# Loading wk in a row on one queue, an earlier activation-table load, and one kv group masked alone, in a gated linear-attention and MLP kernel

## The chip, the cores and the metric

The kernel runs on one NeuronCore of a Trainium2 chip. The metric is the device time of one execution in microseconds (us). A core has five engines that run side by side and meet at semaphores: TensorE (PE, with its weight loads PEld), VectorE (DVE), ScalarE (ACT), GpSimd (POOL) and SyncE (SP). DMAs are issued here by SP and ACT, each in the order of its own instructions, and are carried by 16 DMA engines.

## What is computed

Two branches read the same x (2048 tokens of 640 values) and are mixed by a gate that is one number per token:

```python
g = sigmoid((x * gate_w).sum(-1, keepdims=True))
# A: linear attention, 32 heads of 20; phi(t) = where(t > 0, t + 1, exp(t)) + 1e-6
q, k, v = split(x @ wqkv)
kv = einsum("bhsd,bhse->bhde", phi(k), v);  z = phi(k).sum over tokens
a  = (phi(q) @ kv / (phi(q) . z + 1e-6)) @ wo
# B: LayerNorm, w1, gelu, shifts of channel groups by 1 or 2 tokens, w2, residual;
#    then LayerNorm, w3, gelu, w4, residual
out = g * a + (1 - g) * b
```

Inputs and output are bf16.

## The kernel before

The order of the work on each engine is the order in which the program is written (a manual schedule): nothing is moved by a planner. Semaphore waits follow from the data and from the buffers. TensorE runs through these stages: k projection, q projection, the g products (phi(k) transposed times x), the first part of the MLP with the kv products between, and then, tile by tile of 512 tokens, w2, w3, attention output and w4.

PSUM is handed out in four pairs of banks by `pair()` in turn, so the fifth pair that is asked for takes the place of the first and waits until that one has been read.

**The start.** wk (640 by 640) is loaded in five pieces of 128 rows, wk0 to wk4 (`load_wk`), x in chunks of 128 tokens. The projections need x transposed, `xT`. Chunks 2 to 15 get it from seven transposing DMAs on SP's queue (`load_xT`: chunk 2, chunk 3, then pairs, then the last four). Chunks 0 and 1 are loaded plainly and *turned* on TensorE: `turn(c, dcs, pt, copy)` multiplies pieces of the chunk by the identity into a PSUM pair, from where VectorE or ScalarE copies them into `xT`. VectorE copies pieces 0 and 1 by way of the pair `tp`, ScalarE pieces 2, 3 and 4 by way of the pair `warm`. SP issues x chunk 0, x chunk 1, wk1, wk3 and then the transposes and all later weights; ACT issues the gate weights `g5`, wk0, wk2, wk4, and then loads its activation table, which belongs to a one-element Exp (L208).

On TensorE: five filler matmuls of ones (`warmup`, L204), the gate weights turned (L210, whose result VectorE puts into a spare column of wk), a short filler, the turn of chunk 0 (L217), two more fillers of 512 and 256 columns, the turn of chunk 1, and then the k projection (`k_mm`, L191): for each piece dc of the contraction, two matmuls of 320 columns for chunk 0 and two for chunk 1, into `kps[0]` and `kps[1]`; from chunk 2 on chunk by chunk. `k_evac` takes each result out with ScalarE (L195, L183) and VectorE (L184, L185).

**The kv mask.** `kv_mm` (L428) computes the products for head groups 0 to 2 into one PSUM pair and for groups 3 to 5 into another. `kv_mask` (L436, and L441 for the last, narrower group) multiplies them by a block mask into `kvT` on VectorE, three groups at a time. Then `m_mm` (L450) multiplies groups 0, 1 and 2 of `kvT` by wo, each into a pair of its own, and the MLP's `w1_mm` (L395) follows.

Of the kernel before, what the change touches and what calls it, by code (L numbers as in the profile page):

```python
# [7 lines left out]
ACT = mybir.ActivationFunctionType  # L8
ALU = mybir.AluOpType
BF16 = mybir.dt.bfloat16  # L10
# [6 lines left out]
def kernel(  # L17
# [13 lines left out]
    nc = tc.nc  # L31
    P = 128
# [4 lines left out]
    TS = 512  # L37
    NT = S // TS
    CPT = TS // P
    DC = D // P  # L40
# [8 lines left out]
    GW = GH * Dh  # L49
    NG = 6  # L50
# [17 lines left out]
    def pair():  # L68
        return ps.tile([P, 2, 512], F32, name="pp")
# [28 lines left out]
    gate = const.tile([P, NCH], F32)  # L98
# [20 lines left out]
    sp, aq, gq = nc.sync, nc.scalar, nc.gpsimd  # L119

    def load_x(c0, c1, q=sp):
        q.dma_start(x_sb[:, c0:c1, 0:D], x2[c0 * P:c1 * P, :].rearrange("(c p) d -> p c d", p=P))
# [4 lines left out]
    def load_wk(q, dc):  # L127
        q.dma_start(wk_sb[:, dc, 0:D], A_wqkv[dc * P:(dc + 1) * P, D:2 * D])
# [1 line left out]
    load_x(0, 1)  # L130
    aq.dma_start(g5[:], gate_w.rearrange("(c p) -> c p", p=P))
    load_x(1, 2)
    load_wk(aq, 0)
    load_wk(sp, 1)
    load_wk(aq, 2)
    load_wk(sp, 3)
    load_wk(aq, 4)
    for c0, c1 in ((2, 3), (3, 4), (4, 6), (6, 8), (8, 10), (10, 12), (12, 16)):
        load_xT(c0, c1)
    sp.dma_start(wq_sb, wqkv_v[:, :, 0:D])  # L140
# [7 lines left out]
    for g in (0, 2):  # L148
# [8 lines left out]
                            base=0, pattern=[[-1, P]], channel_multiplier=1)  # L157
    for c in range(0, NCH, CPT):
# [3 lines left out]
                            base=0, pattern=[[-4, H]], channel_multiplier=1)  # L162
    nc.gpsimd.affine_select(out=hmask[:], in_=hmask[:], compare_op=ALU.is_ge, fill=0.0,
                            base=3, pattern=[[4, H]], channel_multiplier=-1)
# [3 lines left out]
                            base=0, pattern=[[-HP, 2], [-Dh, GH], [0, Dh]], channel_multiplier=1)  # L168
    nc.gpsimd.affine_select(out=bmask2[:], in_=bmask2[:], compare_op=ALU.is_ge, fill=0.0,
                            base=Dh - 1, pattern=[[HP, 2], [Dh, GH], [0, Dh]], channel_multiplier=-1)  # L170
# [16 lines left out]
    def k_mm(pt, c, dcs, first=0, last=DC - 1):  # L187
        for dc in dcs:
            for hf in range(2):
                n = HD + hf  # L190
                nc.tensor.matmul(pt[:, hf, 0:n], lhsT=xT[:, dc, c * P:(c + 1) * P],  # L191
                                 rhs=wk_sb[:, dc, hf * HD:hf * HD + n], start=(dc == first), stop=(dc == last))
# [4 lines left out]

    warm, tp = pair(), pair()
    kps = [pair(), pair()]
    one = nc.const_aps.tensor(1.0, (P, TS), BF16)  # L200

    def warmup(n, w=TS, pt=kps[1]):
        for i in range(n):
            nc.tensor.matmul(pt[:, 1, 0:w], lhsT=one[:, 0:P], rhs=one[:, 0:w], start=True, stop=True)  # L204

    nc.vector.memset(g5z[:], 0.0)
    nc.vector.tensor_copy(g5z[0:DC, :], g5[:])
    nc.scalar.activation(gate[:, 0:1], one[:, 0:1], ACT.Exp)  # L208
    warmup(5)
    nc.tensor.matmul(kps[0][:, 0, 0:DC], lhsT=g5z[:], rhs=ident[:, 0:DC], start=True, stop=True)  # L210
    warmup(1, P)
# [2 lines left out]
    def turn(c, dcs, pt, copy):  # L214
        a, n = min(dcs), len(dcs)
        for dc in dcs:
            nc.tensor.matmul(pt[:, 0, (dc - a) * P:(dc - a + 1) * P], lhsT=x_sb[:, c, dc * P:(dc + 1) * P],  # L217
                             rhs=ident[:], start=True, stop=True)
        copy(xT[:, a:a + n, c * P:(c + 1) * P], pt[:, 0, 0:n * P].rearrange("p (c s) -> p c s", c=n))  # L219

    turn(0, (1, 0), tp, nc.vector.tensor_copy)
    turn(0, (2, 3, 4), warm, nc.scalar.copy)
    warmup(1, TS)
    warmup(1, 2 * P)
    turn(1, (1, 0), tp, nc.vector.tensor_copy)
    turn(1, (2, 3, 4), warm, nc.scalar.copy)
    for dc in range(DC):
        for c in range(2):
            k_mm(kps[c], c, (dc,))
    for c in range(2):  # L230
        k_evac(kps[c], c)
    for c in range(2, NCH):
        pt = pair()
# [186 lines left out]
    def kv_mm(g0, g1):  # L420
        pt = pair()
        for g in range(g0, g1):
            for fc in range(DC):
                for v in range(2 if g < NG - 1 else 1):
                    q = 2 * g + v
                    h0, h1 = GH * q, min(GH * (q + 1), H)
                    c1, o = min(GW * q + HP, D), (g - g0) * GW
                    nc.tensor.matmul(pt[HP * v:HP * v + c1 - GW * q, 0, o:o + (h1 - h0) * Dh],  # L428
                                     lhsT=wv_sb[:, fc, GW * q:c1],
                                     rhs=gT[:, fc, 0:D].rearrange("p (j m) -> p j m", j=DC)[:, :, 4 * h0:4 * h1],  # L430
                                     start=(fc == 0), stop=(fc == DC - 1))
        return pt

    def kv_mask(g0, g1, pt):
        n, k = min(g1, NG - 1) - g0, 2 * Dh
        nc.vector.tensor_tensor(  # L436
            kvT[:, g0:g0 + n, 0:GW].rearrange("p g (r j) -> p g r j", j=DC),
            pt[:, 0, 0:n * GW].rearrange("p (g j r) -> p g r j", g=n, j=DC),
            bmask[:].rearrange("p (r j) -> p r j", j=DC).unsqueeze(1).broadcast_to([P, n, 4 * GH, DC]), op=ALU.mult)
        if g1 == NG:  # L440
            nc.vector.tensor_tensor(  # L441
                kvT[0:k, NG - 1, 0:k].rearrange("p (r j) -> p r j", j=DC),
                pt[0:k, 0, n * GW:n * GW + k].rearrange("p (j r) -> p r j", j=DC),
                bmask[0:k, 0:k].rearrange("p (r j) -> p r j", j=DC), op=ALU.mult)
# [24 lines left out]
    hx0 = w1_gelu(0, w1_split[2], w1_mm(0, w1_split[2]))  # L469
    den_hi(halves[1])  # L470
    kv_ps = [kv_mm(0, 3), kv_mm(3, NG)]
    for i in range(2):
        kv_mask(3 * i, 3 * i + 3, kv_ps[i])
    mps = [pair() for _ in range(3)]
    for g in range(3):
        m_mm(g, mps[g])
# [270 lines left out]
```

## Time and profile before

| | us |
|---|---|
| median of 3 runs | 260.62 (260.37 to 261.76) |
| the profiled execution | 261.01 |
| its span, first to last instruction | 259.3 |
| TensorE busy | 254.4 (98% of the span) |
| VectorE, ScalarE, GpSimd busy | 147.5, 108.0, 32.6 |
| first turn, second turn, first k matmul start at | 3.22, 4.37, 4.92 |
| first q matmul starts at | 27.3 |

The profile is of one execution. Times within it count from the start of its span; a line L191 is line 191 of the kernel before. The busy time of an engine counts its instructions, not its waits or its DMA issues. The chain of waits goes back from the last instruction to what released each step. A queue such as SPq shows the issuing of a DMA, not its transfer; the landing time counts from the start of the issue to the completion.

### The profile page before, as it was taken

The page shows a single profiled execution, that of the slowest core. Times are in us where ns is not written, and L with a number is a line of the kernel's source. Part 1 is how long each engine was busy: PE and PEld are TensorE (multiplying, and loading weights), DVE is VectorE, ACT ScalarE, POOL GpSimd, SP SyncE. Part 2 cuts the span into 40 slices and gives each one's busy share as a digit, 9 for nine tenths or more (in the row PEclk, how much of TensorE's full clock was granted, in tenths as well). Part 3 has the DMA queues.
Part 4 walks back from the last instruction along what each step waited for, and adds up shares of the span by engine and source line. Part 5 has one row for each costly group of instructions (what it writes and reads, how often), then busy time and mean ns, then how long its engine had stood idle before and what let it go on. Part 6 is the DMA issues. An engine that isn't in the chain of part 4 may idle for free.

```text
span 259.3 us, 4190 instructions
## 1 busy us (share of the span) xinstructions
PE 254.4 (98%) x1625; PEld 150.5 (58%) x1648; DVE 147.5 (57%) x273; ACT 108.0 (42%) x168; POOL 32.6 (13%) x86
## 2 busy tenths in 40 slices
PE   8999999999999999999999999999999999999995
PEld 4777555688854644565464566464565555465543
DVE  2588778799999987697300497600287610125132
ACT  3555444375797447431342323343321343342100
POOL 4000050023411230041000131000132000000000
PEclk9999999999999999999999999999999999999999
DMA  7999998025572787934011023212022401211011
GB/s 213 188 177 371 355 266 285 11 30 126 126 99 55 118 164 217 309 118 96 3 40 40 20 61 88 78 29 53 20 53 72 101 23 40 57 31 58 18 52 52
DMA packets 57358, 27.98 MB, mean 108 GB/s; under 512 B 45394, under 2 KB 56442, under 8 KB 57338
## 3 DMA queue, kind: packets, MB, share of 16 engines
q1 hardware_dynamic: 56896, 27.22, 42.5%
q10 hardware_dynamic: 442, 0.49, 0.5%
q8 instruction: 13, 0.21, 0.4%
q14 instruction: 7, 0.06, 0.1%
HBM read 12.86 MB, written 3.47 MB: 63 GB/s over the span
## 4 chain that ended last, share of the span: by engine, by line
PE 98%; issue 1%; DVE 0%
PE pp L569 21%; PE pp L608 16%; PE pp L191 9%; PE pp L519 8%; PE pp L340 8%; PE pp L550 8%; PE pp L395 8%; PE pp L242 8%; PE pp L644 5%; PE pp L204 1%; PE pp L579 1%; PE pp L600 1%; PE pp L217 0%; PE pp L450 0%; PE pp L428 0%
## 5 line engine op out<-in xcount | busy, mean ns | idle before, releaser
L569 PE MATMUL pp<-lnxT,w_sb 128*128 128x512 bf16 x249 | 59.8, 379 | 0.6
L571 ACT ACTIVATE h<-pp 128x1024 bf16<-128x1024 f32 (+1 forms) x28 | 26.9, 962 | 56.0 <-PE pp L569 56.0
L608 PE MATMUL pp<-h,w_sb 128*128 128x512 bf16 (+1 forms) x228 | 42.4, 343 | 0.3
L569 PEld LDWEIGHTS <-w_sb 128*128 128x128 bf16 x260 | 25.2, 98 | 26.8
L522 DVE TENSOR_TENSOR x<-pp,x_sb 128x640 f32<-128x640 f32 x16 | 13.1, 816 | 40.6 <-PE pp L519 40.6
L608 PEld LDWEIGHTS <-w_sb 128*128 128x128 bf16 x234 | 22.7, 98 | 19.5 <-issue 1.0
L183 ACT ACTIVATE e<-pp 128x640 bf16<-128x640 f32 (+1 forms) x26 | 21.4, 827 | 9.6 <-PE pp L242 9.6
L303 POOL TENSOR_SCALAR rstd<-mv 128x1 f32<-128x1 f32 (+2 forms) x22 | 9.2, 417 | 127.9 <-DVE mv L309 127.0
L556 DVE SCALAR_TENSOR_TENSOR x<-pp,gate,x 128x640 f32<-128x640 f32 x16 | 14.1, 882 | 18.2 <-PE pp L550 12.6
L550 PE MATMUL pp<-m_sb,pqT 128*128 128x320 bf16 x160 | 24.3, 299 | 0.0
L519 PE MATMUL pp<-w_sb,hsT 128*128 128x320 bf16 x160 | 23.9, 299 | 0.0
L191 PE MATMUL pp<-wk_sb,xT 128*128 128x320 bf16 (+1 forms) x160 | 22.5, 304 | 0.0
L340 PE MATMUL pp<-x_sb,pk 128*128 128x320 bf16 (+1 forms) x160 | 22.0, 300 | 0.0
L242 PE MATMUL pp<-xT,hsT 128*128 128x512 bf16 x98 | 21.6, 379 | 0.1
L340 PEld LDWEIGHTS <-pk 128*128 128x128 bf16 x160 | 18.8, 117 | 3.2
L519 PEld LDWEIGHTS <-hsT 128*128 128x128 bf16 x160 | 15.6, 98 | 8.3 <-issue 0.4
L550 PEld LDWEIGHTS <-pqT 128*128 128x128 bf16 x160 | 15.7, 98 | 7.7
L621 DVE SCALAR_TENSOR_TENSOR oc<-pqT,omg,x 128x640 bf16<-128x640 bf16 x12 | 10.5, 877 | 16.7 <-DMA pqT<-hx 16.7
L191 PEld LDWEIGHTS <-xT 128*128 128x128 bf16 x160 | 15.9, 100 | 6.4 <-DVE xT L219 0.2
L395 PE MATMUL pp<-lnxT,w_sb 128*128 128x512 bf16 x77 | 17.9, 379 | 0.2
L242 PEld LDWEIGHTS <-hsT 128*128 128x128 bf16 x100 | 11.8, 118 | 9.7
L304 POOL TENSOR_TENSOR rstd<-rstd,mhalf 128x1 f32<-128x1 f32 (+2 forms) x22 | 16.8, 762 | 1.8
(93 smaller groups left out, 248.7 us busy)
## 6 DMA issues: line engine op xcount, KB each, us to landing
x_sb<-in_A_x_dram SPq DMA_DIRECT2D x1, 2240.0 KB
out_dram<-oc SPq DMA_DIRECT2D x14, 160.0 KB, 2.0
w_sb<-in_B_w_dram SPq DMA_DIRECT2D x1, 2160.0 KB, 16.8
w_sb<-in_B_w_dram SPq DMA_DIRECT2D x1, 2080.0 KB, 8.9
hsT<-in_A_wqkv_dram SPq DMA_DIRECT2D x1, 800.0 KB, 6.0
m_sb<-in_A_wqkv_dram SPq DMA_DIRECT2D x1, 800.0 KB, 12.4
w_sb<-in_B_w_dram SPq DMA_DIRECT2D x1, 800.0 KB, 11.8
m_sb<-m_dram SPq DMA_DIRECT2D x1, 800.0 KB, 4.3
```

What stands on the lines that cost most here:

```text
L183: nc.scalar.activation(ev, src, ACT.Exp)
L191: nc.tensor.matmul(pt[:, hf, 0:n], lhsT=xT[:, dc, c * P:(c + 1) * P], rhs=wk_sb[:, dc, hf * HD:hf * HD + n], start=(dc == first), stop=(dc ...
L242: nc.tensor.matmul(pt[:, t % 2, :], lhsT=wq_sb[:, dc, :].rearrange("p (m j) -> p j m", j=DC)[:, j], rhs=xT[:, dc, t * TS:(t + 1) * TS], st ...
L304: nc.gpsimd.tensor_tensor(out_ap, out_ap, mhalf[:, 0:out_ap.shape[1]], op=ALU.pow)
L340: nc.tensor.matmul(pt[:, hf, 0:HD + hf], lhsT=w, rhs=x_sb[:, c, hf * HD:(hf + 1) * HD + hf], start=(c == 0), stop=(c == NCH - 1))
L395: nc.tensor.matmul(pt[:, i, :], lhsT=w, rhs=lnxT[t][:, dc, :], start=(dc == 0), stop=(dc == DC - 1))
L519: nc.tensor.matmul(pt[:, hf, 0:HD], lhsT=hsT[:, fc, 2 + c * P:2 + (c + 1) * P], rhs=w2_sb[:, fc, hf * HD:(hf + 1) * HD], start=(fc == 0), ...
L550: nc.tensor.matmul(pt[:, hf, 0:HD], lhsT=pqT[:, j, c * P:(c + 1) * P], rhs=m_sb[:, j, hf * HD:(hf + 1) * HD], start=(j == 0), stop=(j == D ...
L556: nc.vector.scalar_tensor_tensor(x1, pt[:, :, 0:HD], gate[:, c:c + 1], x1, op0=ALU.mult, op1=ALU.add)
L569: nc.tensor.matmul(pt[:, k, :], lhsT=w3_sb[:, dc, fc * P:(fc + 1) * P], rhs=lnT[:, dc, :], start=(dc == 0), stop=(dc == DC - 1))
L571: nc.scalar.activation(h2[:, 2 * i * TS:(2 * i + n) * TS], pt[:].rearrange("p h e -> p (h e)")[:, 0:n * TS], ACT.Gelu_apprx_tanh)
L608: nc.tensor.matmul(dst, lhsT=w4_sb[:, fc, d * P:(d + 1) * P], rhs=st[t]["h2"][:, fc * TS + a:fc * TS + b], start=False, stop=(fc == FF - 1))
```

## The change

At the start: wk0 to wk3 are issued by SP in a row behind x chunks 0 and 1, so that SP's transposes come after six issues instead of four; ACT issues only the gate weights and wk4, and its one-element Exp, with the table load, stands between these two. The two fillers ahead of the second turn are gone. The second turn does its pieces 2, 3, 4 first, by way of `kps[1]` instead of `warm`, and then 1 and 0. The k projection does pieces 0 and 1 of chunk 0, then 0 and 1 of chunk 1, and alternates from piece 2 on.

At the kv mask: the first three groups are masked by two VectorE instructions, group 0 alone and groups 1 and 2 together; `kv_mask` gets the first group of its PSUM pair as `base`.

```diff
     load_x(1, 2)
-    load_wk(aq, 0)
-    load_wk(sp, 1)
-    load_wk(aq, 2)
-    load_wk(sp, 3)
-    load_wk(aq, 4)
+    one = nc.const_aps.tensor(1.0, (P, TS), BF16)
+    nc.scalar.activation(gate[:, 0:1], one[:, 0:1], ACT.Exp)
+    for dc in range(DC - 1):
+        load_wk(sp, dc)
+    load_wk(aq, DC - 1)
...
     kps = [pair(), pair()]
-    one = nc.const_aps.tensor(1.0, (P, TS), BF16)
...
-    nc.scalar.activation(gate[:, 0:1], one[:, 0:1], ACT.Exp)
     warmup(5)
...
     turn(0, (1, 0), tp, nc.vector.tensor_copy)
     turn(0, (2, 3, 4), warm, nc.scalar.copy)
-    warmup(1, TS)
-    warmup(1, 2 * P)
+    turn(1, (2, 3, 4), kps[1], nc.scalar.copy)
     turn(1, (1, 0), tp, nc.vector.tensor_copy)
-    turn(1, (2, 3, 4), warm, nc.scalar.copy)
-    for dc in range(DC):
+    for c in range(2):
+        k_mm(kps[c], c, (0, 1))
+    for dc in range(2, DC):
         for c in range(2):
             k_mm(kps[c], c, (dc,))
...
-    def kv_mask(g0, g1, pt):
+    def kv_mask(base, g0, g1, pt):
         n, k = min(g1, NG - 1) - g0, 2 * Dh
+        c0 = (g0 - base) * GW
         nc.vector.tensor_tensor(
             kvT[:, g0:g0 + n, 0:GW].rearrange("p g (r j) -> p g r j", j=DC),
-            pt[:, 0, 0:n * GW].rearrange("p (g j r) -> p g r j", g=n, j=DC),
+            pt[:, 0, c0:c0 + n * GW].rearrange("p (g j r) -> p g r j", g=n, j=DC),
...
     kv_ps = [kv_mm(0, 3), kv_mm(3, NG)]
-    for i in range(2):
-        kv_mask(3 * i, 3 * i + 3, kv_ps[i])
+    kv_mask(0, 0, 1, kv_ps[0])
+    kv_mask(0, 1, 3, kv_ps[0])
+    kv_mask(3, 3, NG, kv_ps[1])
```

## The prediction

> **What bounds the kernel now.** I read the page first (engine table, chain of waits), then the timeline of the first 24 us engine by engine, the matmuls and weight loads of the first 8 us one by one in very narrow windows, the landing times of the first DMAs, and last the timeline around 77 us, where the kv mask is taken.
>
> ```profile
> span 259.3 us, 4190 instructions
> ...
> PE 254.4 (98%) x1625; PEld 150.5 (58%) x1648; DVE 147.5 (57%) x273; ACT 108.0 (42%) x168; POOL 32.6 (13%) x86
> ...
> PE 98%; issue 1%; DVE 0%
> ```
>
> TensorE carries 98% of the chain that ended last. So an edit is worth only what it takes out of TensorE's own row of work, or out of its gaps, and only two places are touched: the start, and the kv mask. The start, on SP's queue, on ScalarE and on TensorE:
>
> ```profile
> 0.79 0.87 SPq L122 DMA_DIRECT2D x_sb<-in_A_x_dram  x2
> 1.71 0.90 SPq L128 DMA_DIRECT2D wk_sb<-in_A_wqkv_dram  x2
> 2.65 13.11 SPq L125 DMA_TRANSPOSE xT<-in_A_x_dram  x7
> ```
>
> ```profile
> 1.38 1.32 ACTq L128 DMA_DIRECT2D wk_sb<-in_A_wqkv_dram  x3
> 2.73 1.28 ACT L208 ACT_TABLE_LOAD   x1 [2.73 <-issue]
> 4.03 0.20 ACT L208 ACTIVATE gate<-const-bfloat16-1.0 128x1 f32<-128x1 bf16 x1
> 4.14 0.46 ACT L219 CAST xT<-pp 128x384 bf16<-128x384 f32 x1
> ```
>
> ```profile
> 3.22 0.72 PE L217 MATMUL pp<-ident,x_sb 128*128 128x128 bf16 x5
> 3.73 0.85 PE L204 MATMUL pp<-const-bfloat16-1.0 128*128 128x512 bf16 x2
> 4.37 0.76 PE L217 MATMUL pp<-ident,x_sb 128*128 128x128 bf16 x5
> 4.92 19.27 PE L191 MATMUL pp<-wk_sb,xT 128*128 128x320 bf16 x136
> ```
>
> Columns: start, length, engine, line. SP's seven x transposes stand behind four short loads; ScalarE loads its table behind its own DMA issues, and its first copy comes right after. The turn of x chunk 0 runs at 3.22, two fillers at 3.73, the turn of chunk 1 at 4.37, the k projection from 4.92. Its weight loads, one by one, tell the pace of the array:
>
> ```profile
> 5.72 0.15 PEld L191 LDWEIGHTS <-xT 128*128 128x128 bf16 x1
> 5.99 0.15 PEld L191 LDWEIGHTS <-xT 128*128 128x128 bf16 x1
> 6.18 0.10 PEld L191 LDWEIGHTS <-xT 128*128 128x128 bf16 x1
> 6.32 0.10 PEld L191 LDWEIGHTS <-xT 128*128 128x128 bf16 x1
> ```
>
> One step is 0.267 us up to 5.99 and 0.136 us from 6.18; the step between, 0.19, puts the change at about 6.1. So everything before 6.1 ran at half pace, though the granted clock column of the profile stands at full speed throughout. TensorE time saved before 6.1 is therefore worth only 1 - 0.136/0.267 = 0.49 of itself: the k matmuls that move forward into the gap still run at the slow pace.
>
> **The start, part by part.** The *fillers* are 0.43 us (3.73 to 4.16) and 0.21 us (4.16 to 4.37), 0.64 us in all. What is late next is chunk 1: its load was issued at 1.24 and landed 2.6 later, at 3.84 (DMA landing view). The new second turn can start at about 3.87, after a gap of 0.14. Its steps (0.107 each) for pieces 2, 3, 4 come first, to a buffer (kps[1]) that nothing reads; before, they shared *warm* with the first turn and waited for ScalarE's copy (a step of 0.17, from 4.48 to 4.65). Pieces 1 and 0 wait for VectorE's first copy, which runs 3.65 to 4.07, so about 4.19 and 4.30, with the first k matmul at 4.40 instead of 4.92: 0.52 earlier.
>
> *wk on SP.* One issue costs SP 0.42 to 0.43, 0.46 with its gap. wk0 moves from ACT's queue (1.38) to SP's (1.71), wk1 from 1.71 to 2.17, wk2 from 1.78 to 2.63, wk3 from 2.17 to 3.09. The two x loads took 2.4 and 2.6 from issue to landing, the wk pieces 2.9 to 4.0 while two queues mixed them. With 2.6, wk0 lands at 4.31, in time for 4.40; with 2.9, at 4.61, which would leave only 0.31 of the 0.52. I take 2.6: it is the row of the transfer just ahead on the same queue, and the DMA engines already moved 380 to 400 GB/s here, 0.41 us for a piece of 160 KB. wk1 then lands at 4.8 (by the longer row 5.07), and the new order (both pieces of chunk 0, then chunk 1) first asks for it at 4.93: at most 0.14 of slow time. The order also puts chunk 1's first matmul at 5.47, which hides VectorE's copy (4.65 to 5.07) and the added wait for ScalarE's copy of kps[1] (two of 0.46 from about 3.95: done 4.9). wk2 and wk3 are asked for at 6.3 and 6.9 and issued at 2.63 and 3.09: with 4.0 they would be 0.3 and 0.2 late (the gain is gone), with 2.9 they land at 5.5 and 6.0; behind wk1 at 0.41 each, 5.2 and 5.6. I take those.
>
> *Table load.* It takes 1.28 and its activation 0.20, now ahead of wk4's issue: 1.38 + 1.28 + 0.02 + 0.20, so wk4 goes out at 2.9 instead of 2.25 and lands between 5.8 and 6.9. It is the 17th k matmul that reads it, at 7.4: hidden, with 0.5 to spare. What the move frees is ScalarE's first copy, which waited for it (ready by about 3.95, ran at 4.14). In the trace the activation follows the load by 0.02 (4.01 to 4.03). [...]
>
> *x transposes.* All seven stand behind two more issues on SP: first issue 3.57 instead of 2.65, all 0.92 later. The single-chunk one lands 3.8 after its issue, the next (chunks 4, 5) 4.2, then 4.8 and 4.6. Chunk 2: 7.4 against a first read at 8.09 - 0.25 = 7.84. Chunk 3: 8.7 against 9.2. Chunks 4 and 5: issue 6.24, landing 10.44 against a read at 10.82 - 0.25 = 10.57: 0.13 to spare, the tightest. Chunks 6, 7: 12.4 against 13.3; later ones gain room, as SP takes 1.8 us for two chunks and TensorE 2.7. The loads behind them on SP move by 0.92 too: wq lands 22.7, read at 27.5; w1 33.8, and GpSimd's copies of it end at 37, read at 75; w3 48, and SP's next transposes start at 54. All hidden.
>
> Sum of the start: 0.52 x 0.49 = 0.25 us earlier. Ends: nothing (wk0 as late as 4.92), and 0.38, where chunks 4 and 5 stop it, if more were gained.
>
> **The kv mask**, on VectorE, and the next weight load of TensorE behind it:
>
> ```profile
> 76.87 0.35 DVE L436 TENSOR_TENSOR kvT<-pp,bmask 128x180 bf16<-128x180 f32 x1 [0.27 <-PE pp L428]
> 77.30 0.28 DVE L436 TENSOR_TENSOR kvT<-pp,bmask 128x120 bf16<-128x120 f32 x1
> 77.50 0.18 DVE L441 TENSOR_TENSOR kvT<-pp,bmask 40x40 bf16<-40x40 f32 x1
> ```
>
> ```profile
> 77.80 0.11 PEld L395 LDWEIGHTS <-w_sb 128*128 128x128 bf16 x2 [0.25 <-DVE kvT L441]
> ```
>
> TensorE's last kv matmul starts at 77.08, the m matmuls (L450) at 77.27, once the first mask has ended at 77.22. With group 0 alone (60 columns, about 0.2 by the row of 40) they could start near 77.13. But the next w1 unit takes the PSUM pair that the *last* mask (L441) reads, and waits for that: 77.80. The third mask starts at 77.30, when TensorE has drained (77.26), and the new pair of masks, started at 76.87, is issued by about 77.21 (120 columns hold VectorE 0.20, 40 columns 0.11; 60 some 0.13). So L441 ends when it did, the 0.14 won at the front is waited for at 77.8, and I value the edit at nothing. Added wait: the second m matmul now waits for the second mask; behind it stand the third and that w1 unit, which wait for L441 anyway. If VectorE's masks do not overlap (0.21 + 0.28 + 0.28 + 0.18), L441 ends at 77.83 and the edit costs 0.15; if the unit did not wait, it would win 0.09 (m matmuls' end 77.71 against 77.80).
>
> **Sum.** The profiled execution took 261.0 us, its span 259.3 and 1.7 around it. Less 0.25: 260.75. That execution lies 0.4 above the median of the three runs (260.6), so I place the forecast on the median's footing: 260.6 - 0.25 = 260.4.
>
> **The rivals.**
> *The array stays slow for longer (slower).* Place: the gap of 0.14 at 3.73, where the fillers kept TensorE busy. For it: the fast pace came only after TensorE had been busy without a gap over 0.1 since 3.22, that is after 2.88 us. If a gap starts that count again, the change comes at 3.87 + 2.88 = 6.75: 0.65 more slow time, 0.32 lost, +0.07 net, 260.7. If it starts the whole 5.27 us from the first matmul (0.83) again, it comes at 9.14: 3.04 more, 1.49 lost, +1.24 net, 261.9. It decides from a change later than 6.62, where the loss passes 0.25. Against it: a gap of the same size (3.09 to 3.22) lay within the last 3.1 us before the change, and did not prevent it. [...]
> *Chunks 4 and 5 land late.* With the 4.8 of the next pair: 6.24 + 4.8 = 11.04 against the old read at 10.82: +0.22, 260.8. For: only 0.13 to spare. Against: their 4.2 was reached with other loads ahead.
> *The moved issues eat the gain.* wk0 lands at 4.9 or later, or wk2 0.3 late: 260.6. For: the longest landings of the trace. Against: those pieces shared the engines with a second queue.
> *The masks do not overlap.* +0.15 on the forecast: 260.5. Against: L441 was issued 0.20 after a mask that lasted 0.28.
> *More than forecast.* The pace changes before 4.4, and 0.38 counts in full, with 0.09 from the mask: 260.1.
>
> **Chances.** Forecast (260.1 to 260.5) 0.60; array slow for longer 0.14; chunks late 0.09; gain eaten 0.09; masks 0.04; more 0.04. Most lie inside half a per cent (1.3 us, about what a measurement of this kernel can tell from no change). The three runs spread over 1.4 us (260.37 to 261.76), so a median can move by some tenths on its own: range 259.8 to 261.5, which leaves out the far end of the first rival. Slower than 261.9 needs that far end or scatter: 0.10. Faster than 259.3 has no mechanism here, only scatter: 0.04. Within: 0.86.
>
> **What would show it.** Right: turn 2 near 3.87, first k matmul near 4.40, step change still near 6.1, chunk 2's first matmul some 0.25 earlier, no DMA wait at chunks 4 and 5; near 77 a gap ahead of the m matmuls that is smaller, and an equal one behind them. Wrong: a step of 0.267 past 6.6; a TensorE wait on xT or wk_sb; L441 ending more than 0.6 after the last kv matmul's start.

## The result, and the profile after

The changed kernel is slower: 261.68 us, median of 17 runs (260.99 to 263.5), against 260.84 of 17 runs of the kernel before (260.32 to 261.76). The ratio is 1.0046, 95% interval 1.0027 to 1.0065. The forecast was 260.4, its range ended at 261.5. Two executions of a later variant (264.58 and 264.94 us, with the fillers out) count as slow and are left out of its ratios below, but not out of its counts. The profiled execution took 261.67 us, 0.66 more than that of before (261.01). From its page:

```profile
span 259.7 us, 4210 instructions
...
PE 254.8 (98%) x1646; PEld 149.6 (58%) x1646; DVE 147.8 (57%) x274; ACT 108.1 (42%) x168; POOL 32.6 (13%) x86
...
PE 96%; DMA 2%; SPq 1%; issue 0%; DVE 0%
```

TensorE now carries 96% of the chain that ended last; at its start a DMA and SP's queue take its place. The chain of waits in order of time (start, length, what; the small issue gaps left out):

```profile
0.79 0.39 SPq L122
...
1.24 0.42 SPq L122
...
1.71 0.42 SPq L128
...
3.60 5.06 DMA xT<-in_A_x_dram
...
8.70 19.25 PE pp L191 x140
```

SP issues x and the four wk pieces, then the transposing load of chunk 2, which lands 5.06 us after its issue, and only then the k projection goes on. TensorE, and ScalarE's queue, at the start of the changed kernel (L215 are the turns; the third fence has the weight loads of the second turn, before and after):

```profile
3.05 0.73 PE L215 MATMUL pp<-ident,x_sb 128*128 128x128 bf16 x5
4.78 0.45 PE L215 MATMUL pp<-ident,x_sb 128*128 128x128 bf16 x5 [0.99 <-DMA x_sb<-in_A_x_dram]
5.28 3.05 PE L191 MATMUL pp<-wk_sb,xT 128*128 128x320 bf16 x20
8.70 0.58 PE L191 MATMUL pp<-wk_sb,xT 128*128 128x320 bf16 x3 [0.38 <-DMA xT<-in_A_x_dram]
```

```profile
1.38 1.28 ACT L134 ACT_TABLE_LOAD   x1 [1.38 <-PEq L731]
1.45 0.37 ACTq L128 DMA_DIRECT2D wk_sb<-in_A_wqkv_dram  x1
2.68 0.20 ACT L134 ACTIVATE gate<-const-bfloat16-1.0 128x1 f32<-128x1 bf16 x1
3.82 0.48 ACT L217 CAST xT<-pp 128x384 bf16<-128x384 f32 x1 [0.94 <-PE pp L215]
```

```profile
4.16 0.70 PEld L217 LDWEIGHTS <-x_sb 128*128 128x128 bf16 x5 [0.28 <-DMA x_sb<-in_A_x_dram]
...
4.77 0.28 PEld L215 LDWEIGHTS <-x_sb 128*128 128x128 bf16 x5 [1.25 <-DMA x_sb<-in_A_x_dram]
```

Where the fillers were, TensorE stands idle for 0.99 us: chunk 1 landed 3.5 us after its issue, at 4.73, not 2.6. The second turn starts at 4.78 instead of 4.37, the k matmuls at 5.28 instead of 4.92, when wk0 has landed (1.71 + 3.5). In this execution the array is already at full pace at 4.78 (the five weight loads of the turn take 0.28 us instead of 0.70), against 6.1 in the execution of before. That wins part of it back, until chunk 2 is waited for. Chunk 2's first weight load is at 8.70 against 8.09, and the q projection starts at 27.79 against 27.30. From there the two profiles run in parallel, but for the kv mask (VectorE's masks, then TensorE's next weight load):

```profile
77.36 0.22 DVE L435 TENSOR_TENSOR kvT<-pp,bmask 128x60 bf16<-128x60 f32 x1 [0.27 <-PE pp L426]
...
77.79 0.28 DVE L435 TENSOR_TENSOR kvT<-pp,bmask 128x120 bf16<-128x120 f32 x1
77.99 0.18 DVE L440 TENSOR_TENSOR kvT<-pp,bmask 40x40 bf16<-40x40 f32 x1
```

```profile
78.23 0.11 PEld L393 LDWEIGHTS <-w_sb 128*128 128x128 bf16 x2 [0.26 <-DVE kvT L440]
```

The last kv matmul started at 77.58, so the w1 unit follows it by 0.65 instead of 0.72, still behind the last mask.

The executions tell more than the median. Those of before reach from 260.3 to about 262.2 (135 of all 139 taken in this study lie below 262.2; three of the other four are listed with a mean granted clock of 0.993, where all others listed have 0.999 or 1.000, and may have another cause). The changed kernel has 6 of 17 above 262.7 and none below 260.9, where before has 49 of 139. So there are two things to explain: a raised lower end and a second group above.

### The profile page after: what moved, and what is told of

Read it like the earlier page. It is cut to its first block, busy times and chain, and to the rows that moved or that the text cites. A ratio compares the mean times of both kernels' runs of the same rounds, so it can differ in the third digit from the quotient of the medians.

```text
span 259.7 us, 4210 instructions
## 1 busy us (share of the span) xinstructions
PE 254.8 (98%) x1646; PEld 149.6 (58%) x1646; DVE 147.8 (57%) x274; ACT 108.1 (42%) x168; POOL 32.6 (13%) x86
## 4 chain that ended last, share of the span: by engine, by line
PE 96%; DMA 2%; SPq 1%; issue 0%; DVE 0%
PE pp L569 22%; PE pp L608 16%; PE pp L519 8%; PE pp L338 8%; PE pp L550 8%; PE pp L393 8%; PE pp L240 8%; PE pp L191 7%; PE pp L644 5%; DMA xT<-in_A_x_dram 2%; PE pp L579 1%; PE pp L600 1%; SPq L128 1%; PE pp L449 0%; PE pp L426 0%; SPq L122 0%
## 5 line engine op out<-in xcount | busy, mean ns | idle before, releaser
L569 PE MATMUL pp<-lnxT,w_sb 128*128 128x512 bf16 x260 | 60.4, 379 | 0.0
L393 PE MATMUL pp<-lnxT,w_sb 128*128 128x512 bf16 x80 | 18.1, 379 | 0.0
L240 PEld LDWEIGHTS <-hsT 128*128 128x128 bf16 x100 | 11.8, 118 | 9.7
```

What stands on the lines that cost most here:

```text
L240: nc.tensor.matmul(pt[:, t % 2, :], lhsT=wq_sb[:, dc, :].rearrange("p (m j) -> p j m", j=DC)[:, j], rhs=xT[:, dc, t * TS:(t + 1) * TS], st ...
L393: nc.tensor.matmul(pt[:, i, :], lhsT=w, rhs=lnxT[t][:, dc, :], start=(dc == 0), stop=(dc == DC - 1))
L569: nc.tensor.matmul(pt[:, k, :], lhsT=w3_sb[:, dc, fc * P:(fc + 1) * P], rhs=lnT[:, dc, :], start=(dc == 0), stop=(dc == DC - 1))
```

## The experiments

Two theories, stated ahead of the runs. **Gap:** without the fillers TensorE idles, and in some executions the fast pace comes later, so that these take 1 us or more longer. **Queue:** wk in a row on SP lands later, and TensorE waits for it. All executions; the last column is the ratio to the executions of before taken beside them on the same chip, with its 95% interval:

| kernel | executions | lowest | median | above 262.2 | ratio to before |
|---|---|---|---|---|---|
| before | 139 | 260.32 | 261.18 | 4 | |
| changed | 17 + 12 | 260.99 | 261.68 | 6 + 5 | 1.0046 [1.0027, 1.0065]; 1.0033 [1.0010, 1.0055] |
| changed, fillers back | 12 | 261.10 | 261.56 | 0 | 1.0010 [0.9991, 1.0029] |
| changed, old queues | 12 | 261.05 | 261.90 | 4 | 1.0040 [1.0011, 1.0069] |
| before, wk row on SP only | 12 + 12 | 260.88 | 261.37 | 0 | 1.0009 [0.9992, 1.0026]; 0.9996 [0.9973, 1.0018] |
| before, fillers out only | 12 + 12 | 260.36 | 261.31 | 5 + 5 | 1.0016 [0.9990, 1.0041]; 1.0006 [0.9972, 1.0040] |
| before, turns + k order + mask | 12 + 12 | 260.40 | 261.31 | 2 + 0 | 1.0018 [0.9994, 1.0043]; 0.9993 [0.9978, 1.0009] |
| before, mask only | 12 | 260.26 | 260.87 | 0 | 0.9992 [0.9977, 1.0008] |
| before, table load only | 12 | 261.27 | 261.59 | 2 | 1.0005 [0.9979, 1.0030] |
| before, no filler at all | 10 | 261.28 | 262.60 | 7 | 1.0040 [1.0008, 1.0071] |

The median of before itself moved from 260.84 to 261.50 between comparisons, so lowest times and counts say more across rows than medians do.

**Fillers back in the changed kernel.**

```diff
+    warmup(1, TS)
+    warmup(1, 2 * P)
     turn(1, (2, 3, 4), kps[1], nc.scalar.copy)
```

> The changed kernel with the two fillers put back ahead of its second turn; all else as changed. Gap theory (without fillers TensorE stands idle while x chunk 1 is on its way, and in some executions the fast pace comes one interval later): the executions near 263 us vanish, and the median falls by 0.3 us or more, to 261.4 or below with before at 260.8. Queue theory (wk in a row on SP lets x chunk 1 and the first transposes land late, and TensorE waits for them in every execution): chunk 1 still lands near 4.8 us, chunk 2's first k matmul starts near 8.7, and the median stays 0.6 to 0.9 above before.

```profile
3.61 0.85 PE L203 MATMUL pp<-const-bfloat16-1.0 128*128 128x512 bf16 x2
4.25 0.68 PE L215 MATMUL pp<-ident,x_sb 128*128 128x128 bf16 x5
5.10 0.43 PE L191 MATMUL pp<-wk_sb,xT 128*128 128x320 bf16 x2 [0.17 <-DMA wk_sb<-in_A_wqkv_dram]
6.02 3.16 PE L191 MATMUL pp<-wk_sb,xT 128*128 128x320 bf16 x22 [0.49 <-DMA wk_sb<-in_A_wqkv_dram]
```

The group above 262.2 is gone (0 of 12), as the gap theory said. The median, 261.56, did not fall to 261.4 as it had said, and the lowest time stayed at 261.1: TensorE still waits for wk, 0.17 and 0.49 in this profile. Chunk 1 landed 2.6 after its issue here, with the same queue, where the queue theory had it near 4.8, so its lateness is not the queue's doing.

**Old queues in the changed kernel** (the five wk loads are issued as before; nothing else is undone).

> The changed kernel with wk0, wk2, wk4 on ACT and wk1, wk3 on SP as before; table load, turns, order of the k matmuls, missing fillers and masks as changed. Queue theory: chunk 1 lands near 3.8 us again, the gap ahead of the second turn shrinks from 1.0 to about 0.15, chunk 2 is not waited for, and the time is 0 to 0.3 us below before. Gap theory with any gap harmful: still some executions 1 us or more above the others, median 0.3 us or more above before.

Missed by the queue theory: 4 of 12 above 262.2, and the lowest time did not fall. The run does not settle the theory, since the table load still stands ahead of ACT's issues: of three, the third went out only at 3.08 (the table-load experiment below has the same). But the longest wait of its profile (262.05 us) is another one, for wk1 on SP's queue, which landed 4.8 after its issue; the wait for the late piece, wk4, is the last one:

```profile
4.76 0.44 PE L193 MATMUL pp<-wk_sb,xT 128*128 128x320 bf16 x2
6.51 2.07 PE L193 MATMUL pp<-wk_sb,xT 128*128 128x320 bf16 x14 [1.31 <-DMA wk_sb<-in_A_wqkv_dram]
8.76 3.43 PE L193 MATMUL pp<-wk_sb,xT 128*128 128x320 bf16 x24 [0.18 <-DMA wk_sb<-in_A_wqkv_dram]
```

**Only the wk row on SP, in the kernel before.**

> The kernel before with only wk0 to wk3 on SP. Queue theory: chunk 1 lands 0.5 to 1 us later than before, the fillers cover 0.5 of that, the second turn starts near 4.8, chunk 2's transpose is waited for; median 0.4 to 0.9 us above before. Gap theory: the gap behind the fillers is under 0.5 us, too small to put off the fast pace: median within 0.3 us of before, no execution above 262.5.

> Once more the kernel before with only wk0 to wk3 on SP. Two causes: lowest time 0.6 to 0.8 above that of before, none above 262.2, median 0 to 0.6 above before. If the first sample was chance: lowest time near 260.4.

None of 24 above 262.2, one of 24 below 260.9. The lower end is raised by 0.56 (260.88 against 260.32); the median's difference is not resolved. TensorE in the two profiles, the first sample's first:

```profile
4.59 0.45 PE L215 MATMUL pp<-ident,x_sb 128*128 128x128 bf16 x5 [0.54 <-DMA x_sb<-in_A_x_dram]
5.21 0.71 PE L189 MATMUL pp<-wk_sb,xT 128*128 128x320 bf16 x4 [0.17 <-DMA wk_sb<-in_A_wqkv_dram]
6.09 6.16 PE L189 MATMUL pp<-wk_sb,xT 128*128 128x320 bf16 x44 [0.18 <-DMA wk_sb<-in_A_wqkv_dram]
```

```profile
4.36 0.74 PE L215 MATMUL pp<-ident,x_sb 128*128 128x128 bf16 x5
5.43 3.84 PE L189 MATMUL pp<-wk_sb,xT 128*128 128x320 bf16 x27 [0.34 <-DMA wk_sb<-in_A_wqkv_dram]
```

In the first the turn waits for chunk 1, behind the fillers; in the second it is where it was before. In both the k matmuls wait for wk, 0.34 to 0.35 in all, which is most of the 0.56; the rest is not traced. In the five profiles with wk0 on SP it landed 3.3 to 3.7 after its issue at 1.71, at 5.0 to 5.4; in the seven with it as ACT's first piece ahead of the table load, 2.8 to 3.4 after 1.38, at 4.2 to 4.8.

**Only the fillers out, in the kernel before.**

```diff
-    warmup(1, TS)
-    warmup(1, 2 * P)
     turn(1, (1, 0), tp, nc.vector.tensor_copy)
```

> The kernel before with only the two fillers taken out. The second turn then waits for VectorE's copy (about 4.15 us) and, for its last three pieces, for ScalarE's copy (about 4.65), so the k matmuls start near 4.9 as before, with about 0.4 us of gap. Gap theory: some executions are 1 us or more above the others, median 0.2 us or more above before. Queue theory: chunk 1 lands near 3.8, time within 0.2 us of before.

> Once more the kernel before with only the two fillers taken out, for more executions. Two causes: lowest time near 260.4 as before, 30 to 45% of the executions above 262.2, where before has 2 in 81. If the first sample was chance: under 15% above 262.2.

10 of 24 above 262.2 (to 264.94), and 9 of 24 below 260.9, as in before: the lower end is untouched and the upper group is there. This is the gap theory alone. Both of its profiles are of ordinary executions: that of 260.66 us has a gap of 0.59 ahead of the second turn, that of 261.33 two of 0.20 and 0.28. No execution of its upper group was profiled, so that the pace changed late in those is taken from their times.

**The changed kernel once more.** Its profile fell on an execution of 263.6 us.

> The changed kernel itself once more. Two causes: lowest time near 261.0, a part of the executions above 262.2, median 0.6 to 1.2 above before; its profile shows chunk 1 landing 2.6 to 3.5 us after its issue. If the profile falls on one of the slow executions, the step of 0.267 us goes on past 6.6.

TensorE, and its weight loads around 10 us:

```profile
3.14 0.71 PE L215 MATMUL pp<-ident,x_sb 128*128 128x128 bf16 x5
4.57 0.72 PE L215 MATMUL pp<-ident,x_sb 128*128 128x128 bf16 x5 [0.72 <-DMA x_sb<-in_A_x_dram]
5.08 0.74 PE L191 MATMUL pp<-wk_sb,xT 128*128 128x320 bf16 x2
6.22 4.17 PE L191 MATMUL pp<-wk_sb,xT 128*128 128x320 bf16 x15 [0.40 <-DMA wk_sb<-in_A_wqkv_dram]
```

```profile
9.91 0.15 PEld L191 LDWEIGHTS <-xT 128*128 128x128 bf16 x1
10.18 0.14 PEld L191 LDWEIGHTS <-xT 128*128 128x128 bf16 x1
10.36 0.10 PEld L191 LDWEIGHTS <-xT 128*128 128x128 bf16 x1
10.49 0.10 PEld L191 LDWEIGHTS <-xT 128*128 128x128 bf16 x1
```

The step is 0.27 until 10.18 and 0.13 from 10.36: the pace changed near 10.3, after gaps of 0.72 (chunk 1) and 0.40 (wk1). Chunk 2's first weight load comes at 10.49, against 8.70 in the other profile of the same kernel, the q projection starts at 29.70 against 27.79, and the time is 263.6 against 261.67: the 1.9 us of the start are the 1.9 of the whole.

**No filler matmul at all, in the kernel before.**

> The kernel before without any filler matmul, the five at the start included; data and queues as before. Pace theory (the fast pace follows a stretch in which TensorE was busy): the profile shows steps of 0.267 us per 320 columns well past 6.1, the chunk 2 matmuls start 1 us or more later, and the median is 0.8 to 2 us above before. Rival (the fast pace comes at a time of its own, whatever TensorE did): same as the kernel without its two last fillers, lowest time near 260.4 and the fast pace by 6.1.

7 of 10 above 262.2. Weight loads of its profile (264.34 us):

```profile
11.32 0.15 PEld L191 LDWEIGHTS <-xT 128*128 128x128 bf16 x1
11.59 0.15 PEld L191 LDWEIGHTS <-xT 128*128 128x128 bf16 x1
11.83 0.10 PEld L191 LDWEIGHTS <-xT 128*128 128x128 bf16 x1
11.97 0.10 PEld L191 LDWEIGHTS <-xT 128*128 128x128 bf16 x1
```

Without a filler matmul the change of pace comes at about 11.8 here, where the rival (a time of its own, whatever TensorE did) had it by 6.1. In the 16 profiles of the study the four above 263 us have it at 9.9 to 11.8, the twelve below 262.1 by 6.7.

**Only the table load moved, ahead of ACT's three wk issues, in the kernel before.**

> The kernel before with only the table load (and its one-element Exp) moved ahead of ACT's three wk issues. If ACT's issues do not wait for the load (as wk4's, issued at 1.45 during a load from 1.38, in the changed kernel): wk0 and wk2 go out by 1.9, time within 0.3 us of before. If the load holds back later issues (as wk4's at 3.08 with the old queues): wk4 goes out near 3.1, lands late, and the lowest time rises from 260.4 to about 261.0, median 0.2 to 0.7 above before.

ScalarE's queue:

```profile
1.38 1.28 ACT L134 ACT_TABLE_LOAD   x1 [1.38 <-PEq L731]
1.44 0.84 ACTq L128 DMA_DIRECT2D wk_sb<-in_A_wqkv_dram  x2
2.68 0.20 ACT L134 ACTIVATE gate<-const-bfloat16-1.0 128x1 f32<-128x1 bf16 x1
3.15 0.35 ACTq L128 DMA_DIRECT2D wk_sb<-in_A_wqkv_dram  x1
```

Two issues go out while the load runs, the third at 3.15 instead of 2.25, and the 17th k matmul waits 0.57 for that piece at 8.25. The lowest time is 261.27. The changed kernel has only one issue behind the load, at 1.45, so there nothing is held back.

**The new turns, k order and mask alone, in the kernel before.**

> The kernel before with the second turn by way of kps[1] (pieces 2, 3, 4 first), the new order of the k matmuls and the group masked alone; fillers, queues and table load as before. Theory of two causes (missing fillers give the executions above 262.2, wk in a row on SP raises the lowest time from 260.4 to 261.0): neither part is in here, so no execution above 262.2 beyond what before itself shows, lowest time near 260.3, median 0 to 0.3 below before. Rival (the new order of turns and k matmuls is itself a cost, since chunk 1's pieces are asked for earlier): lowest time at 260.8 or above.

> Once more the kernel before with the new second turn, the new order of the k matmuls and the group masked alone, with fillers, queues and table load as before. If these parts cost nothing, as the theory of two causes has it: lowest time near 260.4, at most one execution above 262.2, mean within 0.3 us of before. If the new order is itself a cost: mean 0.4 us or more above before again, and executions above 262.2 again (2 of 12 in the first sample).

The first sample had two above 262.2, the second none, with a ratio of 0.9993: a third cause is not borne out. A gain is not resolved either: against before on the same chip the median is 0.4 above in the first sample and 0.25 below in the second.

**The mask alone.**

> The kernel before with only the first kv group masked alone. By the profile of the changed kernel the w1 unit behind the m matmuls then starts 0.65 us after the last kv matmul instead of 0.72: 0.07 us less, too little for the medians (within 0.2 us of before). Rival (no gain, the last mask sets that start): the distance stays 0.72.

The distance from the last kv matmul to the w1 unit is 0.72 in the seven profiles with the old mask and 0.65 in the nine with the new one. So 0.07 are won, below what the medians can show.

**Two versions meant to be better**, with chunk 1 first on ACT: the gate weights then come second on that queue.

> The turn-and-mask version (fillers kept) with x chunk 1 issued first on ACT, the table load behind the gate weights, and wk0, wk2, wk4 on SP, wk1, wk3 on ACT. If chunk 1's and wk's landing sets the start once the pace is fast: chunk 1 lands near 3.3 us and no k matmul waits for wk more than 0.2 us; lowest time 260.0 to 260.3, median 0.2 to 0.6 below before. If the pace alone sets it: no difference from the turn-and-mask version.

> The turn-and-mask version with x chunk 1 first on ACT and the gate weights second, wk0, wk2, wk4 on SP, wk1, wk3 on ACT, table load behind them, and the gate weights turned on TensorE after the second turn, so that their later landing holds up nothing ahead of it; fillers of 256 columns instead of 128 and of 512 + 256. If the landing of chunk 1 and wk sets the start of executions with an early fast pace: chunk 1 lands by 3.6, lowest time 0.2 to 0.4 below before's lowest, median 0.1 to 0.5 below. If the pace sets it: lowest time and median as before, within 0.2.

Both missed. The gate weights landed late: in the first, their turn on TensorE waited 1.10 (at 4.21 instead of 2.92), and the whole start with it; in the second, the k matmuls waited 0.59 for the wk column made from them. The times: 261.91 to 263.9, ratio 1.0051 [1.0028, 1.0075], and 261.24 to 263.6, ratio 1.0037 [1.0011, 1.0064]. With the gaps the upper group grew (6 of 8, with a raised lower end, and 8 of 12 above 262.2); the one profile of each has the change of pace at 9.9 and 10.2. No version was found that beats both kernels clear of noise; mask alone and turns with mask are level with before.

## Why the prediction was wrong

- **What bounds the kernel**: right. Only the start and the mask mattered, and the start carried through to the end.
- **Chunk 1 at 3.84**: this step failed. I took 2.6 from issue to landing from one execution. In 14 profiles it is 2.5 to 3.5, with either queue order. The fillers of before cover part of that: in the profile with only the mask changed, 0.53 of waiting is left behind them. So the gap is not 0.14 but 0.72 and 0.99 in the two profiles of the changed kernel.
- **The change of pace near 6.1 in both kernels**: this failed too, as it is no fixed time. In the ordinary profiles it came anywhere from 3.5 to 6.7; in 11 of 29 executions of the changed kernel the time (above 262.2 us) says that it came later still, as in the profile of 263.6 us, near 10.3. This is the first rival, given 0.14, and its condition (the gap counts) was dismissed because a gap of 0.13 had been harmless; the real ones, 0.72 and 0.99, were five to eight times as long. The two profiles of the changed kernel also differ in where the gaps fell: the 0.99 from 3.78 came after the change of pace (3.64), the 0.72 and 0.40 in the slow profile ahead of it (10.3). The price of 1.24 was too low: in the changed kernel the executions above 262.2 average 263.18, the others 261.48, so 1.7.
- **wk0 at 4.31**: failed; 5.0 to 5.4. The wk row alone raises the lower end by 0.56, with k matmuls that wait for wk0 or a later piece. My range had kept 4.9 as its end.
- **Half worth of time saved before the change of pace**: right at most where the change is late. In the profiles with an early one, x and wk landing set the start (second turn at 4.43 without the fillers, 4.64 with them, both behind a wait for chunk 1), and there is next to nothing to gain by taking out fillers.
- **Table load**: hidden, as said, but for another reason: wk4's issue, put at 2.9, went out at 1.45, beside the load.
- **Transposes**: chunks 4 and 5 landed at 10.55 (10.44 said) and were not waited for; chunk 2, put at 7.4, was the late one, at 8.66.
- **Mask**: 0.07 won where I said nothing, inside the bounds.

Means of all executions show how the shares add: changed 0.91 above before (262.13 against 261.21), fillers put back 0.28, so 0.6 for the fillers; fillers out alone 0.62, the wk row alone 0.17. The shares rest on a dozen or two executions each and on several comparisons, and by their ratios the last two are not clear of noise; the counts are. What stays open: why chunk 1 lands 2.5 after its issue in one execution and 3.5 in another, where in a given execution the change of pace will fall, and how long a gap ahead of it has to be to put it off. The first two go together: in the six ordinary profiles with the change by 4.6, chunk 1 took 3.15 to 3.49, in the six with a later one 2.54 to 3.15; no run tests why.

## What to carry to other kernels

A filler that covers a DMA can be free even where it looks like work on the bounding engine: here its time would have been idle (0.72 and 0.99 us in two profiles without it), and with the fillers put back 0 of 12 executions were above 262.2, against 11 of 29 without. A landing time from one execution is a sample (2.5 to 3.5 us for the same load here), so a step that needs it within 0.1 us should be priced at the longest row as well. Where executions spread by more than the effect, lowest times and the count above a mark separate causes that the medians leave unresolved.

## What the runs showed of the hardware

The pace of the array at the start is not in the granted clock of the page, which in the profile of before stands at 1.00 in each microsecond from 2 to 8, across the change. The step between weight loads shows it (there 0.267 us until the change and 0.136 after it), and so does the clock record in the packed trace, from which the page takes that column: its first entry, at full clock, starts only at the change. That is at 6.09 in the profile of before, at 3.64 and 10.25 in the two of the changed kernel, at 3.5 to 6.7 in all twelve below 262.1 and at 9.9 to 11.8 in the four above 263. What lies ahead of the first entry is shown as 1.00.

With its table load in the queue, ACT issued three DMAs up to the end of the load, one or two of them while it ran, and the fourth only after the activation behind it (at 3.08, 3.15 and 3.44 in three profiles). In the kernel before, where the load comes last, the fourth went out at 2.25.
